# A fused top-32 attention and gated feed-forward on one core: where the weights are split

## The chip, the cores and the metric

The kernel runs on one core of one Trainium2 chip. The metric is the device time of one execution in microseconds. The core's engines run side by side, each through its own instruction queue in order: TensorE (PE in the profile; PEld is its weight load), VectorE (DVE), ScalarE (ACT), GpSimd (POOL) and SyncE (SP), which here only issues DMAs. An engine that has to wait for another one holds up everything behind it in its queue.

## The reference

For 8 batches, 8 heads, 576 positions and head size 64, the attention keeps the 32 largest scores of each row, takes the softmax over them and multiplies by the values. The result, as 4608 rows of 512, goes through a gated feed-forward part of width 1536.

```python
scores = scale * np.matmul(q, k.transpose(0, 1, 3, 2))
kth = np.partition(scores, -top_k, axis=-1)[..., -top_k:-top_k + 1]
attn = softmax over the scores >= kth          # written out in the reference
x = (attn @ v) as [4608, 512]
gate = 1.0 / (1.0 + np.exp(-(x @ w_gate)))
out = (gate * (x @ w_val)) @ w_out
```

All inputs are float32 or wider; the weights arrive with eight bytes per element, as two 32-bit words.

## The kernel before

**Steps.** The attention runs as 160 steps. A step is one tile of up to 128 query rows for one pair of heads (batch `b`, tile `i`, pair `p`). In batch 0 the tiles are grouped (0, 1), (2, 3), (4): eight steps for the first 256 rows, eight for the next 256, four for the last 64. Step numbers `n` below count from 0. Names in the order carry batch, tile and pair: `e_0_2_0` is batch 0, tile 2, pair 0, step n = 8; `e_0_3_0` is n = 9.

In a step, TensorE makes the scores (`pss`), ScalarE writes them to `s` (L259, L281), VectorE takes the largest eight of each segment (`cand`, L340), narrows them (L344, L346), ScalarE and GpSimd build `under` and `u` (L353, L359), VectorE finds the 32nd largest (`kths`, L367) and masks the exponentials (`e`, L294). TensorE transposes `e` (`pt`), ScalarE writes that to `et` (L384, L392, L401), TensorE multiplies with the values (`po`).

**Iterations.** In iteration n of `run`, PE's code has the scores of step n + 2, the transposes of step n - 2 and the value product of step n - 3; `choose(n)` is the VectorE part of step n. PE's instructions stay in the order in which they are written. For the other engines a scheduler sets the order.

**Feed-forward.** The rows are cut in units, the first three of 256 rows, the others of 384. A unit goes through 18 weight tiles in the list `order` (0, 1, 2, 3, 4, 12, 13, 5, ...): gates (`pz`, L455 to L457) and output products (`po2`, L479 to L481). `more(goal)` runs the unit's matmuls until a number of rows is done. `PACE` and `BEHIND` give that number as a function of the attention's rows: nothing before 256 rows; 24 rows of feed-forward at 256 rows of attention, 272 at 512, 512 at 768, 768 at 1184.

**Splitting.** A weight tile has two halves. `split_front` loads the raw words (`wraw`, L149), and makes from the top and the low word a first part and a fraction: ScalarE L156, L161, L165; VectorE L157 to L159; GpSimd L163 twice. `split_back` lets TensorE form the rest (`wrest`, L172 to L174) in the PSUM pool that the gates use too; ScalarE writes it (L176) and stores the half in DRAM (L177). Later units load the stored tiles. Unit 0 uses the first ten weights of `order` from DRAM (`w_first`) and the last eight straight from the split (`wsplit`).

The first ten weights, 20 halves, are split two halves to an iteration in n = 0 to 9 (`fronts`, L629 to L634 and L673 to L684). From n = 10 on `first_weights` and `next_front` (L187 to L203) split the other 16 halves, every third tick at most (L664 to L668).

Of the kernel before, what the change touches and what calls it, by code (L numbers as in the profile page):

```python
# [10 lines left out]
F32 = mybir.dt.float32  # L11
I32 = mybir.dt.int32
U32 = mybir.dt.uint32
F32R = mybir.dt.float32r
BF16 = mybir.dt.bfloat16
FP8 = mybir.dt.float8e4
AF = mybir.ActivationFunctionType
ALU = mybir.AluOpType
# [11 lines left out]
def tile_topk_attention_then_gated_ffn(  # L30
# [8 lines left out]
    nc = tc.nc  # L39
    P = 128  # L40
    B, H, _, S = k.shape
    D = P // 2
    HALF = S // 2
    NP = H // 2
# [3 lines left out]
    FG = NE = NP  # L48
# [13 lines left out]
    EARLY = 2 * P  # L62
# [14 lines left out]
    PACE = [(EARLY, 24), (2 * EARLY, EARLY + 16), (3 * EARLY, 2 * EARLY), (3 * EARLY + BEHIND, 3 * EARLY)]  # L77

    LOADED = 10
# [46 lines left out]
    for name, bufs in (("w", 3), ("f2", 3), ("f4", NE + 1), ("fg", FG + 2)):  # L126
        pools[name] = ctx.enter_context(tc.tile_pool(name=name, bufs=bufs))
# [10 lines left out]
    pre_pools = {n: pre.enter_context(tc.tile_pool(name=n, bufs=bufs)) for n, bufs in (("signs", 1), ("raw", 3), ("parts", 2))}  # L138
    plus, minus = [pre_pools["signs"].tile([P, P], F32R, tag=t, name=t) for t in ("plus", "minus")]
    nc.scalar.activation(plus, ident, AF.Copy, scale=2.0**-52)  # L140
    nc.scalar.activation(minus, ident, AF.Copy, scale=-1.0)

    def split_front(idx, i):

        if i == 0:
            splits[idx] = pools["w"].tile([P, 2, 2, NP, P], F32R, tag="w", name=f"wsplit_{idx}")
        raw = pre_pools["raw"].tile([P, NP * P, 2], U32, tag="raw", name=f"wraw_{idx}_{i}")
        half = slice(i * NP * P, (i + 1) * NP * P)
        nc.sync.dma_start(raw.rearrange("p n t -> p (n t)"), w[idx][:, half].bitcast(U32))  # L149
        low, top = raw[:, :, 0], raw[:, :, 1]  # L150
        pair = splits[idx][:, i].rearrange("p a c n -> p a (c n)")
        lead = pre_pools["parts"].tile([P, NP * P], F32, tag="lead", name=f"wt_lead_{idx}_{i}")
        frac = pair[:, 1]
        lead_u = lead.bitcast(U32)
        with first_scores(idx == i == 0):
            nc.scalar.activation(lead, top.bitcast(F32), AF.Copy, scale=2.0**-112)  # L156
        nc.vector.tensor_scalar(lead_u, lead_u, 3, None, op0=ALU.logical_shift_left)  # L157
        nc.vector.scalar_tensor_tensor(top, top, 0x80000000, lead_u, op0=ALU.bitwise_and, op1=ALU.bitwise_or)
        nc.vector.tensor_scalar(lead_u, top, 0xFF800000, None, op0=ALU.bitwise_and)  # L159
        with first_scores(idx == i == 0):  # L160
            nc.scalar.activation(frac, low, AF.Copy)  # L161
        for c in (slice(0, 2 * P), slice(2 * P, 4 * P)):
            nc.gpsimd.tensor_tensor(frac[:, c], frac[:, c].bitcast(F32), lead[:, c], op=ALU.mult)  # L163
        bits = top.bitcast(F32)
        nc.scalar.activation(pair[:, 0], bits, AF.Copy)  # L165
        waiting.append((idx, i, pair, bits, ticks[0]))
# [354 lines left out]
    def run(general):  # L521
# [109 lines left out]
        for n in range(len(steps) + 3):  # L631
# [3 lines left out]
            if not general and n == LOADED:  # L635
                first_weights(0)
# [19 lines left out]
            else:  # L656
# [26 lines left out]
                if splitting:  # L683
                    split_back()  # L684
# [77 lines left out]
```

## Time and profile before

| | us |
|---|---|
| median of 3 runs | 1614.03 |
| lowest and highest | 1612.47, 1614.16 |
| the profiled execution | 1610.78 |
| its span | 1608.9 |
| PE busy in the span | 1533.2 (95%) |
| DVE, ACT, POOL busy | 1290.7, 1168.9, 1128.9 |

The span runs from the first instruction to the last. Idle time of PE counts only if PE sets the end in that stretch, so the profile is read by stretches: the opening up to the first gate matmul (0 to 141 us), the rest of batch 0 (to 281 us), a stretch after it (to 455 us), and the long remainder.

### The profile page before, as it was taken

To read this page: it belongs to the slowest core of one execution; us is meant where nothing else is said; L and a number is where in the kernel's file an instruction comes from. 1 tells how busy PE (TensorE), PEld (TensorE's weight loads), DVE (VectorE), ACT (ScalarE), POOL (GpSimd) and SP (SyncE) were. 2 spreads that over 40 slices of the span, in tenths; PEclk is the share of its full clock that TensorE was granted. 3 is DMA by queue.
4 is the path that set the end of the run, shared out by engine and by line. 5 is a ranking of instruction groups with operands and counts; after the bars stand their busy time and mean duration, and the time that the engine had idled before them with its cause. 6 is when DMAs were issued, how large, how long until landed. Compare 5 with 4: busy or idle time off the path is not lost.

```text
span 1608.9 us, 36757 instructions
## 1 busy us (share of the span) xinstructions
PE 1533.2 (95%) x11810; PEld 1428.9 (89%) x11810; DVE 1290.7 (80%) x5940; ACT 1168.9 (73%) x2567; POOL 1128.9 (70%) x1747
## 2 busy tenths in 40 slices
PE   5778998989999999999999999999999999999998
PEld 2346877989999999999999999999999999999998
DVE  7997776799999878799989878799989788899101
ACT  6876787778877777877777777877767777777321
POOL 4765796688886885787776885787776886675322
PEclk9888999999999999999999999999999999999999
DMA  8667587776665665565655665565555665555575
GB/s 250 206 198 272 204 286 280 264 250 226 230 212 201 211 238 198 192 225 200 212 207 180 226 229 195 209 225 204 192 200 204 220 217 180 194 195 182 175 278 191
DMA packets 92459, 348.18 MB, mean 216 GB/s; under 512 B 10336, under 2 KB 37472, under 8 KB 63328
## 3 DMA queue, kind: packets, MB, share of 16 engines
q1 hardware_dynamic: 87072, 326.87, 59.0%
q10 hardware_dynamic: 5184, 18.88, 3.0%
q8 instruction: 95, 1.56, 0.4%
q14 instruction: 108, 0.88, 0.2%
HBM read 317.39 MB, written 28.31 MB: 215 GB/s over the span
## 4 chain that ended last, share of the span: by engine, by line
PE 74%; DVE 12%; ACT 4%; POOL 3%; issue 2%; DMA 1%; POOLq 0%; DVEq 0%; ACTq 0%; SPq 0%
PE pz L455 11%; PE pz L457 11%; PE pz L456 11%; PE pss L273 8%; PE po L414 8%; PE pt L378 6%; PE po L479 6%; PE po L481 5%; PE po L480 5%; DVE cand L340 3%; DVE e L294 3%; DVE kths L367 2%; POOL u L359 1%; DVE cand L346 1%; ACT under L353 1%
## 5 line engine op out<-in xcount | busy, mean ns | idle before, releaser
L359 POOL TENSOR_TENSOR u<-s,under 128x288 f32<-128x288 f32 x576 | 421.9, 756 | 94.0 <-ACT under L353 89.8
L455 PE MATMUL pz<-xh,w 128*128 128x384 f32 (+1 forms) x1152 | 405.8, 352 | 1.7 <-ACT xh L421 1.7
L340 DVE MAX8 cand<-s 128x8 f32<-128x72 f32 x2304 | 347.5, 217 | 67.8 <-ACT s L281 56.1
L456 PE MATMUL pz<-xl,w 128*128 128x384 f32 (+1 forms) x1152 | 377.0, 327 | 3.0 <-POOL xl L422 3.0
L457 PE MATMUL pz<-xh,w 128*128 128x384 f32 (+1 forms) x1152 | 377.9, 328 | 0.0
L294 DVE SCALAR_TENSOR_TENSOR e<-s,kths,e 128x576 f32<-128x576 f32 x288 | 285.3, 994 | 29.4 <-ACT e L289 28.9
L353 ACT ACTIVATE under<-s,leads 128x576 fp8e4<-128x576 f32 x288 | 222.4, 773 | 102.7 <-DVE leads L344 94.2
L367 DVE MAX8 kths<-u 128x8 f32<-128x584 f32 x288 | 219.1, 761 | 65.9 <-POOL u L360 63.3
L289 ACT ACTIVATE e<-s,st 128x576 f32<-128x576 f32 x288 | 210.4, 771 | 35.8 <-PE pt L378 21.0
L455 PEld LDWEIGHTS pz<-xh,w 128*128 128x128 f32 x1152 | 217.6, 189 | 6.1 <-issue 2.6
L456 PEld LDWEIGHTS pz<-xl,w 128*128 128x128 f32 x1152 | 218.3, 189 | 3.4 <-POOL xl L422 3.4
L467 POOL TENSOR_TENSOR gl<-gf,gh 128x384 fp32r<-128x384 f32 (+1 forms) x156 | 155.1, 995 | 91.4 <-ACT gh L466 88.1
L457 PEld LDWEIGHTS pz<-xh,w 128*128 128x128 f32 x1152 | 217.1, 188 | 0.0
L384 ACT ACTIVATE et<-pt 128x384 f32<-128x384 f32 (+1 forms) x384 | 196.9, 523 | 19.5 <-PE pt L378 13.7
L479 PE MATMUL po<-gh,w 128*128 128x384 f32 (+1 forms) x576 | 203.2, 353 | 0.1
L378 PE MATMUL pt<-ident,e 128*128 128x128 f32 x1152 | 191.5, 276 | 7.3 <-ACT et L384 7.0
L480 PE MATMUL po<-gl,w 128*128 128x384 f32 (+1 forms) x576 | 188.3, 327 | 2.6 <-POOL gl L467 2.6
L481 PE MATMUL po<-gh,w 128*128 128x384 f32 (+1 forms) x576 | 188.5, 327 | 0.0
L414 PEld LDWEIGHTS po<-et,v 128*64 128x64 f32 x1600 | 163.8, 139 | 17.0 <-issue 12.7
L414 PE MATMUL po<-et,v 128*64 128x128 f32 (+1 forms) x1600 | 177.1, 268 | 0.0
L415 PE MATMUL po<-et,v 128*64 128x128 f32 (+1 forms) x1600 | 177.1, 268 | 0.0
L281 ACT ACTIVATE s<-pss 128x576 f32<-128x576 f32 x256 | 165.1, 645 | 8.6 <-PE pss L273 8.3
(110 smaller groups left out, 3457.1 us busy)
## 6 DMA issues: line engine op xcount, KB each, us to landing
w<-ws SPq DMA_DIRECT2D x216, 1024.0 KB, 4.9
v<-in_v_dram SPq DMA_DIRECT2D x68, 320.0 KB, 3.6
wraw<-in_w_dram SPq DMA_DIRECT2D x36, 512.0 KB, 4.4
ws<-wsplit ACTq DMA_DIRECT2D x36, 512.0 KB, 4.4
qraw<-in_q_dram SPq DMA_DIRECT2D x140, 128.0 KB, 3.4
kraw<-in_k_dram SPq DMA_DIRECT2D x56, 288.0 KB, 3.7
w_first<-ws SPq DMA_DIRECT2D x10, 1024.0 KB, 4.9
out_dram<-acc SPq DMA_DIRECT2D x40, 192.0 KB, 4.0
```

The lines of the kernel that those rows point to most:

```text
L294: nc.vector.scalar_tensor_tensor(e[:, j], s[:, j], kth[j], e[:, j], op0=ALU.is_ge, op1=ALU.mult, accum_out=st[:, 4 + j : 5 + j])
L340: nc.vector.max(cand[:, j, 8 * g : 8 * g + 8], s[:, j, g * SEG : (g + 1) * SEG])
L359: nc.gpsimd.tensor_tensor(u[:, j, c], s[:, j, c], under[:, j, c], op=ALU.mult)
L367: nc.vector.max(kths[:, at[j] : at[j] + 8], u[:, j])
L378: nc.tensor.transpose(pt[:, c], ef[:, k0 : k0 + P], ident)
L414: nc.tensor.matmul(po[D:, c], vt[:, 5 + a], et[:, 4 + a, :n], start=a == 0, stop=a == 4)
L455: nc.tensor.matmul(ps[:, R], wt[:, u, 0, d], xh[:, R], start=d == 0, stop=False)
L456: nc.tensor.matmul(ps[:, R], wt[:, u, 0, d], xl[:, R], start=False, stop=False)
L457: nc.tensor.matmul(ps[:, R], wt[:, u, 1, d], xh[:, R], start=False, stop=d == NP - 1)
L479: nc.tensor.matmul(ps[:, R], wts[e // 2][:, e % 2, 0, f], gh[:, R], start=f == 0, stop=False)
L480: nc.tensor.matmul(ps[:, R], wts[e // 2][:, e % 2, 0, f], gl[:, R], start=False, stop=False)
L481: nc.tensor.matmul(ps[:, R], wts[e // 2][:, e % 2, 1, f], gh[:, R], start=False, stop=f == FG - 1)
```

## The change

Ten halves, not 20, are split in the iterations n = 0 to 9, one in each; the other 26 are split while unit 0 runs. Up to three halves may be between front and back. The raw load of a half is issued with the front of the half ahead of it. The first part goes to its own tile `wbits` and no longer back into `wraw`; VectorE's third operation reads the upper 16 bits of it at a stride of two and writes a 16-bit `wpower`, which GpSimd multiplies with. The feed-forward pace becomes 16 rows at 256, 232 at 512, 480 at 768, 768 at 1184. The pools change: `parts` 2 to 3 buffers, `power` 1 new, `fg` 6 to 5. `after` has its lines 11 further down: L168, L173, L176 and L187 there are L156, L161, L165 and L176 here.

```diff
-    PACE = [(EARLY, 24), (2 * EARLY, EARLY + 16), (3 * EARLY, 2 * EARLY), (3 * EARLY + BEHIND, 3 * EARLY)]
-    LOADED = 10
+    PACE = [(EARLY, 16), (2 * EARLY, EARLY - 24), (3 * EARLY, 2 * EARLY - 32), (3 * EARLY + BEHIND, 3 * EARLY)]
+    LOADED = 5
-    for name, bufs in (("w", 3), ("f2", 3), ("f4", NE + 1), ("fg", FG + 2)):
+    for name, bufs in (("w", 3), ("f2", 3), ("f4", NE + 1), ("fg", FG + 1)):
...
-        raw = pre_pools["raw"].tile([P, NP * P, 2], U32, tag="raw", name=f"wraw_{idx}_{i}")
-        half = slice(i * NP * P, (i + 1) * NP * P)
-        nc.sync.dma_start(raw.rearrange("p n t -> p (n t)"), w[idx][:, half].bitcast(U32))
+        at = halves_of_weights.index((idx, i))
+        for ahead in halves_of_weights[at : at + 2]:
+            if ahead not in raws:
+                load_raw(*ahead)
...
-        nc.vector.scalar_tensor_tensor(top, top, 0x80000000, lead_u, op0=ALU.bitwise_and, op1=ALU.bitwise_or)
-        nc.vector.tensor_scalar(lead_u, top, 0xFF800000, None, op0=ALU.bitwise_and)
+        nc.vector.scalar_tensor_tensor(word, top, 0x80000000, word, op0=ALU.bitwise_and, op1=ALU.bitwise_or)
+        nc.vector.tensor_scalar(power.bitcast(U16), heads, 0xFF80, None, op0=ALU.bitwise_and)
...
-            nc.gpsimd.tensor_tensor(frac[:, c], frac[:, c].bitcast(F32), lead[:, c], op=ALU.mult)
+            nc.gpsimd.tensor_tensor(frac[:, c], frac[:, c].bitcast(F32), power[:, c], op=ALU.mult)
...
-            if not general and n == LOADED:
+            if not general and n == NP * len(groups[0][1]) + 2:
...
-                        if due and ticks[0] % 3 == 0:
+                        if due and len(waiting) < 3:
                             next_front()
...
-                    if t == 2 and splitting:
-                        if len(waiting) > splitting:
-                            split_back()
-                        if splitting:
-                            split_front(*fronts.pop(0))
+                    if t == 2 and splitting and len(waiting) > 1:
+                        split_back()
...
-                if splitting:
-                    split_back()
```

ScalarE's queue at the very start, in the order before. `s` is the scores of the first two steps, `wraw_1_0` the raw words of the third half; what an instruction waits for stands in brackets:

```order
L259 ACTIVATE s_0_1_0_186<-pss_0_1_0_0_187 128x2x288 [waits PE_49]
L156 ACTIVATE wt_lead_0_0_198<-wraw_0_0_196 128x512 [waits DMAHW5_49]
L161 ACTIVATE wsplit_0_195<-wraw_0_0_196 128x512
L259 ACTIVATE s_0_1_0_186<-pss_0_1_0_1_191 128x2x288 [waits PE_49]
L353 ACTIVATE under_0_0_0_231,sums_0_0_0_228<-s_0_0_0_177,leads_122 128x576 [waits DVE_49,Activation_49]
L165 ACTIVATE wsplit_0_195<-wraw_0_0_196 128x512 [waits DVE_49]
L353 ACTIVATE under_0_0_0_231,sums_0_0_0_228<-s_0_0_0_177,leads_122 128x576
L289 ACTIVATE e_0_0_0_229<-s_0_0_0_177,st_0_0_0_227 128x576 [waits Pool_49]
L289 ACTIVATE e_0_0_0_229<-s_0_0_0_177,st_0_0_0_227 128x576
L156 ACTIVATE wt_lead_0_1_275<-wraw_0_1_273 128x512 [waits DMAHW6_49]
L161 ACTIVATE wsplit_0_195<-wraw_0_1_273 128x512
L161 ACTIVATE wsplit_1_294<-wraw_1_0_295 128x512 [waits DMAHW7_49]
```

The same place of ScalarE's queue in the changed kernel:

```order
L270 ACTIVATE s_0_1_0_189<-pss_0_1_0_0_190 128x2x288 [waits PE_49]
L168 ACTIVATE wbits_0_0_203<-wraw_0_0_199 128x512 [waits DMAHW5_49]
L173 ACTIVATE wsplit_0_198<-wraw_0_0_199 128x512
L173 ACTIVATE wsplit_1_363<-wraw_1_0_283 128x512 [waits DMAHW7_49]
L270 ACTIVATE s_0_1_0_189<-pss_0_1_0_1_194 128x2x288 [waits PE_49]
L364 ACTIVATE under_0_0_0_237,sums_0_0_0_234<-s_0_0_0_180,leads_122 128x576 [waits DVE_49,Activation_49]
```

The instruction that needs the third half's raw words stood eight places behind the second eviction of `s_0_1_0`; now it stands right ahead of it.

TensorE's queue in unit 0, at the gates of weight 4, the fifth of `order`, before:

```order
L455 MATMUL pz_0_1_0_0_1803<-xh_0_0_730,w_first_4_1647 128x256
L456 MATMUL pz_0_1_0_0_1803<-xl_0_0_731,w_first_4_1647 128x256
L457 MATMUL pz_0_1_0_0_1803<-xh_0_0_730,w_first_4_1647 128x256
L455 MATMUL pz_0_1_0_0_1803<-xh_0_1_988,w_first_4_1647 128x256
L456 MATMUL pz_0_1_0_0_1803<-xl_0_1_989,w_first_4_1647 128x256
L457 MATMUL pz_0_1_0_0_1803<-xh_0_1_988,w_first_4_1647 128x256
L378 MATMUL pt_0_2_1_0_1811<-ident_105,e_0_2_1_1414 128x128 x3
```

And in the changed kernel, where weight 12, the sixth, is being split there:

```order
L466 MATMUL pz_0_1_0_0_1688<-xh_0_0_659,w_first_4_1498 128x256
L467 MATMUL pz_0_1_0_0_1688<-xl_0_0_660,w_first_4_1498 128x256
L468 MATMUL pz_0_1_0_0_1688<-xh_0_0_659,w_first_4_1498 128x256
L183 MATMUL wrest_12_0_1692<-wbits_12_0_1546,ident_105 128x512
L184 MATMUL wrest_12_0_1692<-wsplit_12_1543,minus_166 128x512
L185 MATMUL wrest_12_0_1692<-wsplit_12_1543,plus_165 128x512
L266 MATMUL pss_0_2_3_1_1710<-k_0_3_6_378,q_0_2_3_1248 128x288 x2
L466 MATMUL pz_0_1_0_0_1688<-xh_0_1_884,w_first_4_1498 128x256
```

Weight 12, the sixth of `order`, is now the first that is split in use; before it was weight 8, the eleventh. Counted over the whole order, PE's rows up to the first gate matmul are the same but for 30 `wrest` matmuls fewer (30 instead of 60). From there to the last transposes of batch 0 (step n = 19) there are 30 more (78 instead of 48) and 66 gate matmuls fewer (309 instead of 375).

## Rows read from the trace of the kernel before

**Rows 1.** The page: busy time of each engine (share of the span) xinstructions.

```profile
PE 1533.2 (95%) x11810; PEld 1428.9 (89%) x11810; DVE 1290.7 (80%) x5940; ACT 1168.9 (73%) x2567; POOL 1128.9 (70%) x1747
```

**Rows 2.** Windows: stretch and length, busy time by engine, granted clock, DMA share, GB/s.

```profile
0.00:20.00 20.00, 6.65 (x20) 2.54 (x20) 10.40 (x65) 11.77 (x22) 5.99 (x23) 1.00 0.88 251
20.00:141.00 121.00, 86.50 (x411) 46.83 (x412) 111.94 (x464) 96.03 (x189) 82.02 (x119) 0.82 0.67 226
141.00:281.00 140.00, 130.58 (x986) 109.39 (x987) 104.81 (x391) 105.05 (x229) 100.68 (x145) 1.00 0.73 255
281.00:341.00 60.00, 60.00 (x597) 58.94 (x596) 49.90 (x254) 48.19 (x119) 43.17 (x77) 1.00 0.73 260
341.00:455.00 114.00, 104.47 (x974) 100.04 (x973) 107.36 (x551) 93.51 (x214) 96.87 (x154) 0.99 0.67 233
455.00:1590.00 1135.00, 1131.90 (x8756) 1098.42 (x8755) 902.99 (x4215) 812.82 (x1795) 798.14 (x1231) 1.00 0.60 208
```

**Rows 3.** By line: duration ns min/median/max, first and last start, forms.

```profile
L157 DVE TENSOR_SCALAR wt_lead<-wt_lead x36: 401/454/920, 13.3 to 244.9; 128x512 uint32<-128x512 uint32 x36
L158 DVE SCALAR_TENSOR_TENSOR wraw<-wraw,wt_lead x36: 667/738/1228, 13.8 to 245.4; 128x512 uint32<-128x512 uint32 x36
L159 DVE TENSOR_SCALAR wt_lead<-wraw x36: 401/437/922, 14.5 to 246.1; 128x512 uint32<-128x512 uint32 x36
...
L163 POOL TENSOR_TENSOR wsplit<-wsplit,wt_lead x72: 720/736/1295, 15.1 to 251.0; 128x256 fp32r<-128x256 f32 x72
```

**Rows 4.** The page's groups: GpSimd with a one-byte second operand: busy, mean ns.

```profile
L359 POOL TENSOR_TENSOR u<-s,under 128x288 f32<-128x288 f32 x576 | 421.9, 756 | 94.0 <-ACT under L353 89.8
```

**Rows 5.** Timeline of PE around the first gate matmul: start, length, instruction, idle before.

```profile
129.25 2.08 PE L172 MATMUL wrest<-wraw,ident 128*128 128x512 f32 x2 [6.06 <-DVE wraw L158]
...
139.40 0.87 PE L378 MATMUL pt<-ident,e 128*128 128x128 f32 x6
140.20 0.76 PE L255 MATMUL pss<-k,q 64*128 64x288 f32 x4
140.89 0.55 PE L378 MATMUL pt<-ident,e 128*128 128x128 f32 x3
141.27 0.27 PE L381 MATMUL pt<-ident,inv 128*128 128x128 f32 x1
141.30 0.36 PE L455 MATMUL pz<-xh,w_first 128*128 128x256 f32 x1
```

**Rows 6.** Timeline of DVE: the second mask of step n = 8 (`e_0_2_0`).

```profile
108.31 0.81 DVE L294 SCALAR_TENSOR_TENSOR e<-s,kths,e 128x576 f32<-128x576 f32 x1
```

**Rows 7.** Timeline of ACT at the start.

```profile
11.95 0.65 ACT L161 ACTIVATE wsplit<-wraw 128x512 fp32r<-128x512 uint32 x1
12.93 0.65 ACT L259 ACTIVATE s<-pss 128x576 f32<-128x576 f32 x1 [0.32 <-PE pss L255]
```

**Rows 8.** The raw loads issued in the first 20 us: third issue, then landing times.

```profile
L149 SPq DMA_DIRECT2D wraw<-in_w_dram x3: 430/432/583, 3.7 to 9.5; - x3
...
DMA to landing us min/median/max: 4.5/6.3/7.4
```

**Rows 9.** Timeline of PE at 190 us: one half's rest between gate matmuls.

```profile
189.84 0.28 PE L456 MATMUL pz<-xl,w_first 128*128 128x256 f32 x1
189.96 0.28 PE L457 MATMUL pz<-xh,w_first 128*128 128x256 f32 x1
190.08 1.06 PE L172 MATMUL wrest<-wraw,ident 128*128 128x512 f32 x2
190.55 0.82 PE L173 MATMUL wrest<-wsplit,minus 128*128 128x512 f32 x1
191.21 0.40 PE L174 MATMUL wrest<-wsplit,plus 128*128 128x512 f32 x1
191.44 0.28 PE L455 MATMUL pz<-xh,wsplit 128*128 128x256 f32 x1
```

**Rows 10.** Timeline of ACT: transposes of steps n = 9 and n = 19 written out.

```profile
156.61 0.57 ACT L384 ACTIVATE et<-pt 128x512 f32<-128x512 f32 x1
...
281.08 0.56 ACT L401 ACTIVATE et<-pt 64x128 f32<-64x128 f32 x2
```

**Rows 11.** The longest of PE's waits from 141 to 281 us: total, times, longest.

```profile
PE wrest L174 <- POOL wsplit L163: 3.2, 3, 2.0
PE po L480 <- POOL gl L467: 1.5, 1, 1.5
```

**Rows 12.** ACT's operations of a half, 20 to 141 us: xcount, busy us, mean ns, idle before.

```profile
L165 ACT ACTIVATE wsplit<-wraw 128x512 fp32r<-128x512 f32 x19 | 12.9, 679 | 8.2 <-DVE wraw L158 8.2
L156 ACT ACTIVATE wt_lead<-wraw 128x512 f32<-128x512 f32 x19 | 12.8, 674 | 6.0 <-POOL wsplit L163 5.6 <-DMA wraw<-in_w_dram 0.4
L176 ACT ACTIVATE wsplit<-wrest 128x512 fp32r<-128x512 f32 x20 | 11.9, 593 | 0.2 <-PE wrest L174 0.2
L161 ACT ACTIVATE wsplit<-wraw 128x512 fp32r<-128x512 uint32 x17 | 11.5, 679 | 2.3 <-DMA wraw<-in_w_dram 2.0 <-issue 0.2
```

More of the change, by code (lines that the diff above doesn't have):

```diff
@@ L13 @@
 U32 = mybir.dt.uint32
+U16 = mybir.dt.uint16
 F32R = mybir.dt.float32r
@@ L137, in tile_topk_attention_then_gated_ffn @@
     pre = ExitStack()
-    pre_pools = {n: pre.enter_context(tc.tile_pool(name=n, bufs=bufs)) for n, bufs in (("signs", 1), ("raw", 3), ("parts", 2))}
+    pre_pools = {n: pre.enter_context(tc.tile_pool(name=n, bufs=bufs)) for n, bufs in (("signs", 1), ("raw", 3), ("parts", 3), ("power", 1))}
     plus, minus = [pre_pools["signs"].tile([P, P], F32R, tag=t, name=t) for t in ("plus", "minus")]
@@ L141, in tile_topk_attention_then_gated_ffn, with load_raw @@
     nc.scalar.activation(minus, ident, AF.Copy, scale=-1.0)
+    halves_of_weights = [(t, i) for t in order for i in range(2)]
+    raws = {}
+    def load_raw(idx, i):
+        raws[idx, i] = raw = pre_pools["raw"].tile([P, NP * P, 2], U32, tag="raw", name=f"wraw_{idx}_{i}")
+        nc.sync.dma_start(raw.rearrange("p n t -> p (n t)"), w[idx][:, i * NP * P : (i + 1) * NP * P].bitcast(U32))
     def split_front(idx, i):
@@ L146, in split_front @@
             splits[idx] = pools["w"].tile([P, 2, 2, NP, P], F32R, tag="w", name=f"wsplit_{idx}")
-        raw = pre_pools["raw"].tile([P, NP * P, 2], U32, tag="raw", name=f"wraw_{idx}_{i}")
-        half = slice(i * NP * P, (i + 1) * NP * P)
-        nc.sync.dma_start(raw.rearrange("p n t -> p (n t)"), w[idx][:, half].bitcast(U32))
+        at = halves_of_weights.index((idx, i))
+        for ahead in halves_of_weights[at : at + 2]:
+            if ahead not in raws:
+                load_raw(*ahead)
+        raw = raws[idx, i]
         low, top = raw[:, :, 0], raw[:, :, 1]
         pair = splits[idx][:, i].rearrange("p a c n -> p a (c n)")
-        lead = pre_pools["parts"].tile([P, NP * P], F32, tag="lead", name=f"wt_lead_{idx}_{i}")
+        bits = pre_pools["parts"].tile([P, NP * P], F32, tag="bits", name=f"wbits_{idx}_{i}")
         frac = pair[:, 1]
-        lead_u = lead.bitcast(U32)
+        word = bits.bitcast(U32)
+        power = pre_pools["power"].tile([P, NP * P], BF16, tag="power", name=f"wpower_{idx}_{i}")
+        heads = bits.bitcast(U16).rearrange("p (n t) -> p n t", t=2)[:, :, 1]
         with first_scores(idx == i == 0):
-            nc.scalar.activation(lead, top.bitcast(F32), AF.Copy, scale=2.0**-112)
-        nc.vector.tensor_scalar(lead_u, lead_u, 3, None, op0=ALU.logical_shift_left)
-        nc.vector.scalar_tensor_tensor(top, top, 0x80000000, lead_u, op0=ALU.bitwise_and, op1=ALU.bitwise_or)
-        nc.vector.tensor_scalar(lead_u, top, 0xFF800000, None, op0=ALU.bitwise_and)
+            nc.scalar.activation(bits, top.bitcast(F32), AF.Copy, scale=2.0**-112)
+        nc.vector.tensor_scalar(word, word, 3, None, op0=ALU.logical_shift_left)
+        nc.vector.scalar_tensor_tensor(word, top, 0x80000000, word, op0=ALU.bitwise_and, op1=ALU.bitwise_or)
+        nc.vector.tensor_scalar(power.bitcast(U16), heads, 0xFF80, None, op0=ALU.bitwise_and)
         with first_scores(idx == i == 0):
@@ L162, in split_front @@
         for c in (slice(0, 2 * P), slice(2 * P, 4 * P)):
-            nc.gpsimd.tensor_tensor(frac[:, c], frac[:, c].bitcast(F32), lead[:, c], op=ALU.mult)
-        bits = top.bitcast(F32)
+            nc.gpsimd.tensor_tensor(frac[:, c], frac[:, c].bitcast(F32), power[:, c], op=ALU.mult)
         nc.scalar.activation(pair[:, 0], bits, AF.Copy)
```

## The prediction

> **What bounds the kernel now.** I read the engines' shares first, then the busy time by stretches, then the timelines at the stretches' borders and PE's waits. PE is busy for 95% of the span [rows 1], but that is an average. By stretches [rows 2]: from 455 to 1590 us PE is busy for 1131.9 of 1135 us, and nothing there can be won. All else lies ahead of it. From 0 to 141 us PE is busy for 6.7 + 86.5 us and idle for 48; VectorE, at 111.9 of the 121 us after the first 20, is the bound. From 141 to 281 us PE is busy for 130.6 of 140 and sets the pace, with 9.4 us of waits. From 281 to 341 us it is never idle. From 341 to 455 us PE (104.5 of 114) and VectorE (107.4) share the bound, and PE is idle for 9.5 us. At the border, PE waits 6.06 us for VectorE's part of a late half, and the first gate matmul starts at 141.30 [rows 5], although the mask of step n = 8, the last attention result that stands ahead of it in PE's order, was done at 109.1 [rows 6]. So the splits, not the attention, opened the feed-forward part.
>
> The sums are made against the profiled execution, 1610.78 us, which lies 3.25 under the median of the runs, 1614.03. Its span is 1608.9; the 1.9 around it is left as it is.
>
> **The opening.** A half costs VectorE 0.45 + 0.74 + 0.44 = 1.63 us [rows 3]. In the new order 11 halves instead of 16 stand ahead of the second mask of n = 8: 5 x 1.63 = 8.2 us less. Some VectorE work of the following step is drawn ahead of it, though; over all rows up to that mask, by kind and duration, I count 4 us less.
>
> Against it stands the start. In ScalarE's queue the instruction that needs the third raw load has moved ahead of the second eviction of step 1. The load is issued at 9.5 us in a full DMA queue (share 0.88) and lands up to 7.4 us later, near 16.9 [rows 2, 8]. As many loads are ahead of it as before. ScalarE was free for that eviction at 12.6 and ran it at 12.93 [rows 7]; it would now run at about 17. Behind the waiting instruction are that eviction, `under` and the first exponentials; VectorE waits for the eviction and GpSimd for `under`. Cost 4 us, bounds 0 (should the load land early) and 5.
>
> So the mask of n = 8 stays at about 109.1. From there PE has the transposes, a score block and the last weight's rest that stands ahead anyway: 1.9 us at full clock [rows 5], 4 at half. I add 2 for ScalarE's further waits for raw loads, which the scheduler moved early as well. First gate matmul at 115: **26 us earlier than 141.3**.
>
> **What is not done yet by then.** PE's rows up to that point differ by 30 `wrest` matmuls, ten halves. At full clock a half takes 191.44 - 190.08 = 1.36 us of PE [rows 9]: 13.6 us that now lie in a stretch where PE is the bound. In exchange the slower pace leaves out 66 gate matmuls up to the end of batch 0. They start 0.12 us apart (189.84, 189.96) [rows 9]: 7.9 us less.
>
> **New waits.** VectorE's rows from the mask of n = 8 to that of n = 9 come to 10.7 us, so that one is done near 121 to 123. PE has 16 rows of feed-forward until then, 16 x 432 / 256 = 27 matmuls or 3.2 us. It waits 5 us (0 to 8). In the rest of batch 0 PE's 9.4 us of waits belong to 16 halves in use; the longest is for GpSimd's product of a half [rows 11]. With 26 halves, in proportion, 5.9 us more. But half of the weights had their second half's rest directly ahead of their first use, and now at least 2.4 us of other PE work stands between. I take 3 (bounds -3 and 9).
>
> **The sum up to the end of batch 0.** The transposes of n = 19 were out at 281.6 [rows 10]. Now 281.6 - 26.2 + 13.6 - 7.9 + 5 + 3 = 269.1: **12.5 us earlier**.
>
> **What is owed.** The 7.9 us of gates are made up until 1184 rows. Seven rows, 1.4 us, fall to 281 to 341 us, where PE has no idle time: paid in full. The other 6.5 us fall where PE is idle for 9.5 us but VectorE is 94% busy [rows 2]; I let half be hidden, 3.2 (bounds 0 and 6.5). Owed: 4.6.
>
> Net -12.5 + 4.6 = -7.9 us: 1602.9 in the profiled execution's terms, **1606** as a median.
>
> **Edits taken at nothing.** VectorE's third operation, 512 two-byte words read at a stride of two, is not in the trace. Its nearest rows are the one-input operations at 0.40 to 0.45 us and the two-input one at 0.74 [rows 3]; I take 0.44, since it too has one tensor input. At 0.74 it costs 0.3 x 36 = 11 us of VectorE, of which 4 lie in the opening on the path; the rest has VectorE's idle 35 us of the 140 as cover. At 0.40 it gains 0.5 there. GpSimd's product with a two-byte operand: 736 ns for 256 columns with four-byte operands [rows 3], 756 for 288 with a one-byte one [rows 4], so 0.67 to 0.74; no change, covered by GpSimd's 39 us of idle time in 141 to 281. `wbits` apart from `wraw` changes no length and frees the raw buffer earlier; if the raw tile were late still, it is ScalarE's wait counted above. One `fg` buffer less: a buffer comes back five gate tiles later, when PE has at least one tile (24 matmuls, 2.9 us) behind its last reader; without that cover up to 3 us for each of the early reuses. On SP the second raw load now stands ahead of the next pair's keys and queries; they come later by at most the spread of the landings, 2.9 us [rows 8], and PE then waits for ScalarE in any case.
>
> **The clock.** From 20 to 141 us the granted clock is 0.82, from 141 on 1.00: both levels, 1.2 and 2.4 GHz, occur in the opening [rows 2]. With ten rests fewer, at some 2 us each there, PE would be busy for 66 of 95 us, 70%, against 71% now: I expect the same mixture. The Trainium skill ("TensorE: Matmul & The Clock Gate", Part 1, on the clock gate) says that the throttled level is the default and activity releases it. By that, fewer matmuls between gaps speak against the change; by the trace so far only the share of busy time can be compared.
>
> **Rivals.**
> - *ScalarE's queue sets the rest of batch 0 (slower).* A half costs it 0.68 + 0.67 + 0.59 + 0.68 = 2.6 us [rows 12]. It was busy for 105 of the 140 us; ten halves more make 131, in the 154 us from 115 to 269: 85%. Nowhere in rows 2 does it pass 82%. Were 80% its limit, the end of batch 0 is at 115 + 164 = 279, only 2.6 us earlier, and with all 7.9 us owed paid the kernel is 5 us slower: 1619. It decides once ScalarE's work passes about 80% of that stretch. Against it: its idle time there is mostly waiting for others, and it never was the bound.
> - *The opening keeps its length.* ScalarE meets each early raw load before the attention's evictions, as at the start, two or three more times at up to 3 us. The feed-forward opens near 122 and the net is about -1: 1613.
> - *The opening falls to 1.2 GHz throughout (slower).* 66 us of PE at 0.82 become 108, 13 more than the 95 there are: net +5, 1619. For it: less work for each step; against it: the unchanged busy share.
> - *The waits do not come.* No wait for the mask, none added in use, the debt hidden: -7.9 - 8 - 3.2 = -19, 1595.
>
> **How the numbers follow.** What cannot be told from no change is 0.2%, 3.2 us; the three runs span 1.7. Forecast 0.42 (0.37 faster, 0.04 same, 0.01 slower); no waits 0.12, all faster; opening unchanged 0.18 (0.03, 0.12, 0.03); ScalarE 0.20 (0, 0.03, 0.17); clock 0.08 (0, 0.01, 0.07). Together faster 0.52, same 0.20, slower 0.28. The forecast's own range, from the bounds of the waits, the debt and VectorE's third operation, is 1597 to 1614. To leave out no more than 2 in 10 it reaches to the slower rivals: 1597 to 1620.
>
> **What would show it.** The eviction at 12.93 is late by 4 us and waits for a raw load. The first gate matmul starts near 115, with 30 `wrest` matmuls ahead of it. The last transposes of batch 0 are out near 269. PE's idle time between the first gate matmul and there is some 17 us, for masks and halves. From 341 to 455 us its idle time is halved. From 500 us on both traces run alike, shifted. It is wrong if the first gate matmul comes after 125, if ScalarE or GpSimd is the name on most of PE's new waits for over 15 us, or if the end of batch 0 is not earlier than 281.

## The result and the profile after

The changed kernel takes **1595.92 us** (median of 4 runs, 1595.09 to 1597.74), the kernel before 1613.53 beside it: a ratio of 0.9893, 95% interval 0.9876 to 0.9910, or 17.6 us less. A second set of runs gave 0.9901 (0.9887 to 0.9915). The forecast was 1606, with a range from 1597 to 1620: the direction was right, the size was not.

The profiled execution has a span of 1595.9 us. The page's first row answers to [rows 1]: TensorE has the same 11810 instructions and is busy 10.6 us less.

```profile
PE 1522.6 (95%) x11810; PEld 1427.3 (89%) x11810; DVE 1285.6 (81%) x5940; ACT 1165.3 (73%) x2567; POOL 1124.2 (70%) x1747
```

The windows, cut at the first gate matmul, the end of batch 0 and steps n = 27 and n = 40, with the columns of [rows 2] (length, busy time of PE, PEld, DVE, ACT, POOL, granted clock, DMA share, GB/s):

```profile
0.00:20.00 20.00, 5.73 (x18) 2.46 (x20) 6.96 (x45) 6.51 (x11) 2.51 (x18) 1.00 0.89 234
20.00:111.80 91.80, 62.61 (x378) 36.25 (x377) 89.83 (x429) 75.95 (x153) 58.15 (x91) 0.89 0.52 180
111.80:265.90 154.10, 140.53 (x993) 113.10 (x992) 127.97 (x460) 127.86 (x274) 124.33 (x179) 0.98 0.73 253
265.90:324.60 58.70, 58.70 (x574) 57.76 (x573) 47.83 (x253) 47.79 (x120) 40.25 (x72) 1.00 0.74 265
324.60:439.70 115.10, 109.50 (x1029) 106.38 (x1028) 108.31 (x552) 92.18 (x214) 98.78 (x156) 0.99 0.73 253
439.70:1577.00 1137.30, 1132.53 (x8756) 1098.66 (x8756) 901.34 (x4201) 813.50 (x1797) 798.10 (x1233) 1.00 0.59 207
```

In the second row VectorE is idle for 2.0 us of 91.8; before, it was idle for 9.1 of 121 [rows 2]. In the third, TensorE is idle for 13.6 us. A profiled execution of the second set (changed_again) has the same points at 111.8, 264.7 and 438.3 us, so 1 to 2 us between two kernels at such a point say nothing. The next rows are TensorE's around the first gate matmul, which came at 141.30 before [rows 5], and VectorE's second mask of n = 8, which began at 108.31 [rows 6]:

```profile
111.79 0.27 PE L392 MATMUL pt<-ident,inv 128*128 128x128 f32 x1
111.82 0.36 PE L466 MATMUL pz<-xh,w_first 128*128 128x256 f32 x1
...
102.30 1.25 DVE L305 SCALAR_TENSOR_TENSOR e<-s,kths,e 128x576 f32<-128x576 f32 x1
```

This mask is done at 103.55, where it was done at 109.12. From 20 us to there, before and then after:

```profile
20.00:109.12 89.12, 65.21 (x278) 33.93 (x278) 86.09 (x348) 73.74 (x145) 63.02 (x90) 0.83 0.62 207
```

```profile
20.00:103.55 83.55, 54.57 (x315) 30.81 (x313) 81.58 (x385) 71.25 (x144) 55.57 (x85) 0.90 0.54 187
```

ScalarE's start answers to [rows 7]. The copy that needs the third raw load waits 5.64 us, and the eviction behind it starts at 18.90 instead of 12.93:

```profile
12.03 0.66 ACT L173 ACTIVATE wsplit<-wraw 128x512 fp32r<-128x512 uint32 x1
18.34 0.66 ACT L173 ACTIVATE wsplit<-wraw 128x512 fp32r<-128x512 uint32 x1 [5.64 <-DMA wraw<-in_w_dram]
18.90 0.64 ACT L270 ACTIVATE s<-pss 128x576 f32<-128x576 f32 x1
```

VectorE's third operation, on two-byte words at a stride, takes 426 ns in the median; 0.44 was taken, from [rows 3]:

```profile
L171 DVE TENSOR_SCALAR wpower<-wbits x36: 398/426/946, 14.6 to 241.9; 128x512 uint16<-128x512 uint16 x36
```

And the last transposes of batch 0, at 281.08 before [rows 10], are written out at

```profile
265.37 0.55 ACT L412 ACTIVATE et<-pt 64x128 f32<-64x128 f32 x2
```

So the profiled execution gains 15.7 us up to the end of batch 0, keeps 15.4 of it at n = 40 (439.7 against 455.1), and loses 2.4 in the rest of the span.

### The profile page after: what moved, and what is told of

It reads as the page before. It is cut to its first block, busy times and chain, and to the rows that moved or that the text cites. A ratio compares the mean times of both kernels' runs of the same rounds, so it can differ in the third digit from the quotient of the medians.

```text
span 1595.9 us, 36725 instructions
## 1 busy us (share of the span) xinstructions
PE 1522.6 (95%) x11810; PEld 1427.3 (89%) x11810; DVE 1285.6 (81%) x5940; ACT 1165.3 (73%) x2567; POOL 1124.2 (70%) x1747
## 4 chain that ended last, share of the span: by engine, by line
PE 69%; DVE 10%; ACT 3%; POOL 2%; issue 2%; DMA 1%; SPq 0%; ACTq 0%; POOLq 0%; DVEq 0%
PE pz L466 10%; PE pz L468 10%; PE pz L467 10%; PE pss L284 8%; PE po L425 7%; PE pt L389 6%; PE po L490 5%; PE po L492 5%; PE po L491 5%; DVE cand L351 3%; DVE e L305 2%; DVE kths L378 2%; DVE cand L357 1%; PE pt L400 1%; ACT under L364 1%
## 5 line engine op out<-in xcount | busy, mean ns | idle before, releaser
L300 ACT ACTIVATE e<-s,st 128x576 f32<-128x576 f32 x288 | 210.5, 771 | 34.3 <-PE pt L389 18.8
L425 PEld LDWEIGHTS po<-et,v 128*64 128x64 f32 x1600 | 160.4, 137 | 16.5 <-issue 11.6
L425 PE MATMUL po<-et,v 128*64 128x128 f32 (+1 forms) x1600 | 173.5, 265 | 0.0
L426 PE MATMUL po<-et,v 128*64 128x128 f32 (+1 forms) x1600 | 173.5, 265 | 0.0
L389 PEld LDWEIGHTS pt<-ident,e 128*128 128x128 f32 x1152 | 146.0, 141 | 30.4 <-ACT et L395 12.7
```

The lines of the kernel that those rows point to most:

```text
L389: nc.tensor.transpose(pt[:, c], ef[:, k0 : k0 + P], ident)
L425: nc.tensor.matmul(po[D:, c], vt[:, 5 + a], et[:, 4 + a, :n], start=a == 0, stop=a == 4)
```

## The experiments

Four parts were taken apart: the **placement** (five weights, one half per step), the **split** (words and power in tiles of their own, load ahead, one gate buffer less), the **pace** table, and the **rule in use** (fewer than three in flight). All ratios are to the kernel before on the same chip; the medians come from several chips, on which the kernel before had 1611.7 to 1613.5. "Gate" is the first gate matmul, "batch 0" the last transposes of batch 0 (n = 19), both as points of time, and "28-39" the time between the last transposes of n = 27 and of n = 40. All three are from the run's profiled execution.

| kernel | gate | batch 0 | 28-39 | median us | ratio (95%) |
|---|---|---|---|---|---|
| before | 141.3 | 281.6 | 114.1 | 1613.5 | 1 |
| changed | 111.8 | 265.9 | 115.1 | 1595.9 | 0.9893 (0.9876-0.9910) |
| changed_again | 111.8 | 264.7 | 114.9 | 1596.2 | 0.9901 (0.9887-0.9915) |
| place_alone | 111.0 | 283.4 | 113.5 | 1611.5 | 0.9996 (0.9987-1.0005) |
| pace_alone | 140.0 | 280.9 | 115.0 | 1609.2 | 0.9980 (0.9969-0.9992) |
| split_alone | 129.4 | 275.1 | 115.8 | 1603.1 | 0.9943 (0.9926-0.9959) |
| place_pace | 111.7 | 278.6 | 119.7 | 1606.6 | 0.9968 (0.9956-0.9980) |
| old_place | 128.6 | 264.1 | 119.9 | 1597.4 | 0.9910 (0.9896-0.9923) |
| old_place_14 | 128.6 | 262.3 | 115.1 | 1592.5 | 0.9874 (0.9857-0.9890) |
| old_pace | 111.9 | 274.4 | 113.2 | 1602.3 | 0.9940 (0.9924-0.9957) |
| old_ticks | 112.0 | 266.0 | 115.0 | 1596.4 | 0.9899 (0.9883-0.9916) |
| no_ahead | 111.3 | 263.8 | 116.9 | 1595.7 | 0.9896 (0.9880-0.9911) |
| in_place | 113.2 | 269.4 | 120.8 | 1604.7 | 0.9940 (0.9925-0.9955) |
| bits_two | 114.1 | 269.8 | 115.7 | 1599.1 | 0.9917 (0.9904-0.9930) |
| raw_four | 138.6 | 281.1 | 113.1 | 1608.3 | 0.9972 (0.9962-0.9982) |
| no_stall | 106.6 | 260.0 | 118.8 | 1593.6 | 0.9889 (0.9874-0.9904) |
| no_stall_all | 107.6 | 261.7 | 115.6 | 1592.7 | 0.9878 (0.9864-0.9893) |
| no_stall_no_ahead | 104.8 | 258.3 | 120.1 | 1594.2 | 0.9887 (0.9873-0.9901) |
| no_stall_slower | 107.5 | 263.5 | 120.0 | 1598.3 | 0.9916 (0.9903-0.9929) |
| best_14 | 107.3 | 259.9 | 115.0 | 1591.2 | 0.9870 (0.9854-0.9887) |

**The placement, undone and alone.** old_place puts `LOADED = 10`, the second `split_front` of a step and the old `split_back` calls back into the changed kernel; place_alone takes the same lines of the changed kernel into the one before.

> The changed kernel with only the placement undone: ten weights, two halves in each of the first ten steps, the gates called at step 10, as before; the new form of the split, the raw load one half ahead, three in flight and the slower pace stay. Theory A (how many halves stand ahead of the gates decides, all else is small): the first gate matmul is back near 140 us and the time near that of the kernel before, 1610 to 1616, with the slower pace perhaps 2 above it. Rival B (the new form of the split and the raw loads ahead make the opening short): first gate matmul before 125 us, time 1596 to 1602.

> The kernel before with only the placement changed: five weights, one half per step, the gates called at step 10; old form of the split, no raw load ahead, old pace, old rule in use. Theory A: first gate matmul at 110 to 118 us and the time within 4 us of the changed kernel, 1594 to 1601. Rival B: first gate matmul after 125 us, because raw loads and the split's operations come late, and 1606 to 1614. A third reading (placement opens early, but halves in use at the old rule are late) would show the first gate matmul before 118 us, more than 20 us of waits of TensorE for rests from there to the last transposes of batch 0, and 1600 to 1606.

Theory A, which was the prediction's, fell on both. In old_place theory B has the time (1597.4) but not the opening, which comes at 128.6 and not before 125. place_alone opens the gates at 111.0, as A said, and is not faster: from there to the end of batch 0 it needs 172.4 us. Its windows, and TensorE's two longest waits in the second one (total, times, longest):

```profile
20.00:111.00 91.00, 63.38 (x377) 37.46 (x375) 89.12 (x419) 76.27 (x151) 58.84 (x91) 0.89 0.53 181
111.00:283.40 172.40, 153.65 (x1028) 122.89 (x1029) 130.67 (x459) 130.29 (x278) 125.06 (x179) 0.94 0.71 241
...
PE po L479 <- ACT acc L488: 5.9, 1, 5.9
PE wrest L174 <- POOL wsplit L163: 3.7, 3, 2.4
```

Against the 140.3 us before, that is 32 us more: 13.6 for the ten halves [rows 9], 9.4 of further idle time (18.8 against 9.4) and the rest, 9, at the granted clock of 0.94, since it was 1.00 in that stretch before [rows 2]. All that the early gate won (30.3) goes there. The third reading, late halves, missed as well: TensorE's waits ahead of rests come to 5.9 us there, not to over 20, and the time is 1611.5.

**The split and the pace, alone.** split_alone takes the new `split_front`, its pools and `fg` into the kernel before, pace_alone only the line `PACE`.

> The kernel before with only the new split: word and power in tiles of their own, three of them, so that a raw buffer is free after VectorE's second operation and not after TensorE's rest; the raw load one half ahead; one gate buffer less. Ten weights, two halves per step, the old pace and the old rule in use stay. Theory S (raw buffers that waited for TensorE are what made the opening long before: the load of raw words waited 28.8 us for TensorE's rests there): first gate matmul near 128.6, as in the run with only the placement undone, so 12 us before 141.3; the end of batch 0 is 270 to 274 and the time 1601 to 1606. Rival T (an earlier opening is given back in full to waits and to a lower clock, as with the placement alone): end of batch 0 within 3 us of 281.6, time 1609 to 1614.

> The kernel before with only the pace table changed. Theory E: nothing changes up to 141 us; 66 gate matmuls fewer bring the end of batch 0 from 281.6 to 272 to 275, and the time to 1603 to 1606, since the gates left out are done where TensorE is idle. Rival U (owed gates are paid in full after batch 0): end of batch 0 near 274 but step n = 40 within 2 us of 455.1, time 1610 to 1614.

Theory S held, with the end of batch 0 1.1 us beyond its bounds: the split alone wins 0.57%, 9.2 us. What it frees stands in SyncE's queue, where L149 is the load of raw words. From 20 to 141 us, before and then with the new split at the old placement (old_place), as waiting engine, line, releaser: us in total, times, longest:

```profile
SPq L149 <- PE wrest L172: 28.8, 17, 5.9
SPq L149 <- DVE wt_lead L159: 24.3, 6, 7.6
```

```profile
SPq L149 <- DVE wbits L170: 52.3, 16, 5.9
```

Before, TensorE's rest was the last reader of a raw buffer, so the next load, and with it VectorE, stood behind TensorE's order; now VectorE's own second operation gives the buffer back. These waits are as long in all (53.1 and 52.3 us), but for another engine. With that, the ten weights are through and the gates open at 128.6 instead of 141.3:

```profile
20.00:128.60 108.60, 81.30 (x415) 44.07 (x415) 106.10 (x444) 92.86 (x186) 76.43 (x108) 0.87 0.73 241
```

VectorE is idle for 2.5 us in this window, 9.1 before. That is half of the 12.7 us; the other half is VectorE work that no longer stands ahead of the gates (106.1 us against 111.9), a change of order that these runs do not tell apart from the buffers.

pace_alone is 0.2% faster, too little for theory E and, by 0.8 us, too much for rival U, for which batch 0 also ends too late. There are 66 gate matmuls fewer, yet TensorE is busy almost as long as before (129.7 us against 130.6 [rows 2]), at a lower clock:

```profile
140.00:280.90 140.90, 129.69 (x953) 107.87 (x952) 100.07 (x403) 107.09 (x227) 96.25 (x149) 0.95 0.69 236
```

**The pace and the rule, undone.** One line each: `PACE` as before; `if due and ticks[0] % 3 == 0`.

> The changed kernel with only the pace table undone (24, 272, 512 for the due rows of the first three units instead of 16, 232, 480). The four runs so far let theory A fall: the placement alone opens the gates at 111 us and wins nothing, since from there to the last transposes of batch 0 TensorE needs 172.4 us instead of 140.3. Theory E (the slower pace takes 66 gate matmuls, 7.9 us, out of the stretch where TensorE is the bound and they cost nothing later, where TensorE is idle anyway): the end of batch 0 is 8 us or more later than 265.9, 274 to 280, step n = 40 some 6 to 10 us later than 439.7, and the time 1602 to 1606. Rival F (the gates only fill waits): end of batch 0 within 3 us of 265.9, time 1595 to 1599.

> The changed kernel with only the rule in use undone: a new half is begun every third tick instead of whenever fewer than three are in flight. Theory G (three in flight is what spares TensorE the waits for halves in use): TensorE's idle time from the first gate matmul to the last transposes of batch 0 rises from 13.6 us to 18 or more, the end of batch 0 is 5 us or more later, and the time 1600 to 1606. Rival H (the rule hardly matters, since a half needs more than three ticks anyway): the same stretch within 3 us of 154.1, time 1595 to 1599.

Beside the new split the pace is worth 8.5 us at the end of batch 0 and 6 to 8 in all: E held here, as it did not alone. With the old split it brings the end of batch 0 forward by 4.8 us at the new placement (place_alone 283.4, place_pace 278.6) and by 0.7 at the old one. The rule in use does nothing (rival H).

**The load ahead** (`halves_of_weights[at : at + 1]`):

> The changed kernel with the raw words loaded in the step that splits them, not one half ahead. The third raw load still has 15 transfers ahead of it, so the stall at the start stays. Theory A: the splits of the opening stand behind a step of VectorE work and the loads are hidden anyway: first gate matmul within 2 us of 111.8; in use a load that takes 4.5 to 7.4 us comes late for some halves, 1 to 4 us more of waits by TensorE up to the end of batch 0; time 1596 to 1600. Rival D (the load ahead is what keeps VectorE busy): VectorE idle for over 8 us between 36 and 113 us, first gate matmul after 118, time 1603 or more.

It does nothing either: the gates open where A said, and the 1 to 4 us of further waits that A expected do not come (1595.7).

**Both pieces of the prediction together, without the split**: place_pace, the kernel before with the new placement and pace.

> The kernel before with the new placement and the new pace table, but the old split and the old rule in use. Theory S (the new split is needed where halves are split in use, too; the old one makes them late and TensorE's clock drop): first gate matmul at 111, the end of batch 0 not before 274, time 1604 to 1609. Rival V (placement and pace are enough together, as the prediction had it): end of batch 0 at 266 to 270, time 1596 to 1600.

Theory S held, V fell: 0.32% faster of the 1.07%. Its profiled execution took 1612.9 us, 6.3 more than the median of its seven runs (1604.3 to 1612.9). The opening and the rest of batch 0 in it:

```profile
20.00:111.70 91.70, 60.83 (x376) 34.61 (x375) 89.83 (x420) 76.27 (x151) 58.92 (x91) 0.96 0.53 180
111.70:278.60 166.90, 150.05 (x991) 119.06 (x992) 127.58 (x466) 130.03 (x274) 125.54 (x179) 0.92 0.69 232
```

In the second window TensorE's waits ahead of a half's rest come to 14.5 us; they are 9.6 in the changed kernel and 13.7 in in_place, below. Twice such a wait and a fall of the clock come one behind the other. Two windows, the rows that start the falls, and between them a third wait:

```profile
170.00:180.00 10.00, 8.71 (x58) 6.43 (x58) 7.01 (x12) 5.02 (x12) 9.43 (x14) 0.66 0.78 294
220.00:230.00 10.00, 10.00 (x33) 7.85 (x32) 6.49 (x22) 6.02 (x12) 8.41 (x12) 0.54 0.35 118
...
170.87 1.88 PE L172 MATMUL wrest<-wraw,ident 128*128 128x512 f32 x2 [1.83 <-DVE gf L465]
206.96 1.17 PE L172 MATMUL wrest<-wraw,ident 128*128 128x512 f32 x2 [2.34 <-ACT wsplit L176]
218.22 1.49 PE L172 MATMUL wrest<-wraw,ident 128*128 128x512 f32 x2 [2.45 <-ACT wsplit L176]
220.50 1.81 PE L273 MATMUL pss<-k,q 64*128 64x288 f32 x3
```

After waits of 1.83 and 2.45 us the granted clock is 0.66 and 0.54 over ten us, the latter close to the lower of its two levels, 1.2 GHz. TensorE is then busy, but for less work. Not every such wait does it: behind the one of 2.34 us the first two matmuls of the rest take 1.17 us, near the 1.06 of [rows 9], and the clock of 200 to 210 us is 1.00.

**Which part of the split.** raw_four gives the kernel before a fourth raw buffer (`("raw", 4)`, `fg` and `bqr` one less); bits_two the changed kernel two word tiles (`("parts", 2)`); in_place holds the raw buffer again:

```
-        nc.vector.scalar_tensor_tensor(word, top, 0x80000000, word, ...)
+        nc.vector.scalar_tensor_tensor(top, top, 0x80000000, word, ...)
...
-        heads = bits.bitcast(U16).rearrange("p (n t) -> p n t", t=2)[:, :, 1]
+        heads = raw.bitcast(U16)[:, :, 3]
...
+        bits = top.bitcast(F32)
```

> The kernel before with four raw buffers instead of three; one gate buffer and one query buffer of the odd batches less make room. The split, the placement, the pace and the rule in use are those of before. Theory S1 (the new split wins by giving raw buffers back early; its other parts win nothing): a fourth buffer does part of the same, loads of raw words wait for TensorE's rests for less than 15 us instead of 28.8 up to 141 us, VectorE's idle time from 20 us to the first gate matmul falls from 9 us to 5 or less, the first gate matmul comes at 128 to 136, and the time is 4 to 9 us lower, 1603 to 1608. Rival S2 (it is the order of VectorE's instructions, or the two-byte operation, that wins): first gate matmul within 3 us of 141.3 and 1610 to 1614.

> The changed kernel with two tiles for the words of a half instead of three. They are free only after TensorE's rest. Theory S1: VectorE (through ScalarE's first copy of a half) waits for TensorE's rests again; first gate matmul 2 to 8 us later than 111.8, TensorE's idle time from there to the end of batch 0 over 16 us, time 1599 to 1606. Rival W (two are enough, since a half needs under two steps from its first copy to its rest): first gate matmul within 1 us, time 1594 to 1598.

> The changed kernel with VectorE's second operation writing the words back over the raw ones, as before, so that a raw buffer is free only after TensorE's rest has read it; the two-byte third operation and its two-byte product, the placement, the pace, the rule in use and the load ahead stay. Theory S1 (giving the raw buffer back early is the part of the new split that counts): loads of raw words wait for TensorE again, for over 30 us in 20 to 111 us; the stretch from the first gate matmul to the end of batch 0 is 160 us or more instead of 154.1, by more waits and a lower granted clock; time 1602 to 1608, near the placement and the pace with the old split, 1606.6. Rival Y (the two-byte operations or the order that comes with them win): time 1594 to 1598.

raw_four is half a hit for S1: VectorE's idle time falls to 4.3 us and the kernel gains 0.28%, but the loads still wait 31.4 us for TensorE and the gate moves by only 2.7 us, which is within rival S2's bounds. bits_two is as S1 said at the gate (2.3 us later) and at its lower end in time; TensorE's idle time did not rise. in_place has S1's time, 8.5 us over the changed kernel, and its waits, but not its reason: the stretch behind the gates takes 156.2 us, not 160, at a clock of 0.99:

```profile
SPq L149 <- PE wrest L184: 48.6, 10, 8.8
...
113.20:269.40 156.20, 140.81 (x988) 110.54 (x987) 125.21 (x450) 127.50 (x270) 120.61 (x176) 0.99 0.72 249
328.70:449.50 120.80, 112.45 (x1027) 108.58 (x1025) 109.77 (x545) 94.42 (x219) 99.25 (x157) 0.96 0.70 242
```

The gates open only 1.4 us later, though the loads wait 48.6 us for TensorE, and only 3.5 to 4.7 us of the 8.5 are there at the end of batch 0. The rest comes from 329 to 450 us, where no weight is split: 120.8 us instead of 115.1.

**An order far behind the change.** That stretch takes 115 to 117 us in some kernels with the new pace and 118.8 to 120.8 in the others. Between the first masks of `e_1_1_0` and `e_2_0_0`, VectorE's order is one and the same, 399 rows, in changed, old_ticks, no_ahead, bits_two, pace_alone and no_stall_all; in old_place, place_pace, in_place, no_stall and no_stall_no_ahead it is another, 410 rows, the same in these five but for a few rows in its first half. no_stall_slower (120.0), with a pace table of its own, has a third. In old_place_14 and best_14 the first number of `PACE` is 14 instead of 16, which gives the first order; best_14 is otherwise no_stall_no_ahead, below.

> The run with only the placement undone (ten weights, two halves per step), and the first number of its pace table 14 instead of 16. That number changes no work, but with it the scheduler's order of VectorE and ScalarE in the second half of batch 1 (steps 28 to 39, where no weight is split) is row for row the changed kernel's. With 16 it was the other one, and that stretch took 119.9 us instead of 115.1. Theory O (that order alone makes 4 to 5 us, and the placement is worth nothing): the stretch takes 115 to 116 us, the end of batch 0 stays near 264, time 1592 to 1595, not above the changed kernel's. Rival (the stretch is long for what was left undone before it, not for its order): the stretch 119 us or more, 1596 to 1599.

> The changed kernel without the stall at the start, with the raw words loaded in the step that splits them, and 14 for 16 as in the run beside it, which gives the changed kernel's order in steps 28 to 39. Theory O: end of batch 0 near 258 as without the 14, steps 28 to 39 in 115 to 116 us instead of 120.1, time 1588 to 1591, the fastest of all. Rival: 1592 to 1595, as without it.

Theory O held in the stretch (115.1 and 115.0 us) and in old_place_14's time; best_14's time, 1591.2, lies just above its bounds. old_place, then old_place_14, each from the gate to the end of batch 0 and in steps 28 to 39:

```profile
128.60:264.10 135.50, 128.42 (x952) 108.33 (x951) 106.81 (x425) 105.99 (x231) 102.35 (x157) 0.95 0.74 254
322.80:442.70 119.90, 111.28 (x1027) 107.42 (x1026) 109.61 (x545) 94.24 (x219) 99.31 (x157) 0.97 0.70 243
```

```profile
128.60:262.30 133.70, 125.84 (x954) 105.01 (x953) 108.18 (x426) 105.65 (x232) 103.40 (x157) 0.99 0.73 258
321.00:436.10 115.10, 109.54 (x1029) 106.39 (x1028) 108.33 (x552) 92.31 (x214) 98.77 (x156) 0.99 0.72 253
```

With the same order behind it, the old placement is not slower than the new one: 1592.5 us, ratio 0.9874. The new placement opens 16.8 us earlier and needs 20.4 more from there (154.1 against 133.7: 14.7 more of busy TensorE and 5.7 of idle). Whether it costs something in the end, the intervals leave open.

**The stall at the start.** no_stall orders one copy behind the eviction; no_stall_all does it for all halves of the opening (`evicted[2 * at - 1]`); no_stall_no_ahead adds to no_stall that a load is not ahead; no_stall_slower adds a slower pace.

```
-        with first_scores(idx == i == 0):
+        with tc.issue_after(evicted[3].ins) if at == 2 else first_scores(idx == i == 0):
             nc.scalar.activation(frac, low, AF.Copy)
```

> The changed kernel with one order added: the ScalarE copy that needs the third raw load is issued only after the second eviction of step 1 has been placed. Theory A (VectorE bounds the whole opening, so what it loses at the start is lost at the gates): the eviction is back at 12.9 us, VectorE's idle 4.58 us ahead of 19.57 is gone, the first gate matmul comes 4 to 5 us earlier, near 107, and the time is 4 to 5 us lower, 1591 to 1592. Rival C (the early step is made up later, because VectorE or GpSimd waits for loads in the next steps): first gate matmul within 1 us of 111.8, time 1595 to 1597.

> The changed kernel in which each ScalarE copy that needs a raw load in the opening is issued behind the second eviction of the step two ahead. Theory A2 (every wait of ScalarE for a raw load there moves the gates): both waits are gone, the 5.64 us at 18.34 and the 1.99 us at 32.62, the first gate matmul comes at 105 to 107, the end of batch 0 near 260 and the time is 1 to 3 us under the changed kernel's, 1592 to 1595. Rival Z (the copies are now late for GpSimd's product, and TensorE waits for it): first gate matmul after 108, time 1595 to 1599.

> The changed kernel without the stall at the start and with the raw words loaded in the step that splits them. The load ahead made no difference by itself (1595.7 without it). If that holds without the stall as well: first gate matmul at 106 to 108, time 1592 to 1595. If the stall had hidden the late loads: first gate matmul after 109, time 1595 to 1599.

> The changed kernel without the stall at the start and with a pace slower still: 8, 192 and 432 due rows for the first three units instead of 16, 232 and 480, so some 70 gate matmuls fewer up to the end of batch 0. Theory E2 (what is put off still finds idle time of TensorE from 319 to 437 us, 8.2 us there): end of batch 0 at 250 to 254 instead of 260.0, step n = 40 at 431 to 436, time 1587 to 1591. Rival X (that idle time is VectorE's to give and is used up): end of batch 0 near 252, step n = 40 within 2 us of 437.5 and time 1592 to 1596.

Without the stall the gate comes 5.2 us earlier and the end of batch 0 5.9. no_stall then gives 3.7 back by the other order (118.8), and its time misses theory A's by 1.6 us; no_stall_all, whose gate at 107.6 is 0.6 later than its theory had it, keeps the first order and wins 3.4 us over changed_again on the same chip. no_stall_no_ahead opens the gates at 104.8, earlier than expected, has the other order as well (120.1) and its time as expected. no_stall_slower misses both its theories and loses 4 to 5 us on no_stall: with fewer gates to do, batch 0 ends 3.5 us later, and TensorE is idle for 17.6 us from the gates to there (14.1 in no_stall). So the loss is there before anything that was put off is done; its cause was not traced. best_14 is the fastest, 1591.2 us, and beats the kernel before by 1.3%; its interval overlaps one of the changed kernel's two and touches the other, so the 4 to 5 us between the medians are likely, not shown; old_place_14 is no different from it.

## Why the prediction was wrong

- **The step that failed** is "Edits taken at nothing": `wbits` apart from `wraw` "changes no length and frees the raw buffer earlier", and stood in the sum with nothing. The split that it belongs to is the largest single gain: 9.2 us alone. Beside the placement and the pace it takes the ratio from 0.9968 (place_pace) to 0.9893 and 0.9901, which is 11 to 12 us; in the profiled executions 4.6 of them are the order in steps 28 to 39 (119.7 against 115.1). I costed the lengths of operations, not whose order a buffer waited for. How much of it is the buffer is shown in part: in_place undoes that alone, and batch 0 ends 3.5 to 4.7 us later.
- *Where it counts*: at the old placement ahead of the gates, at the new one behind them. With the old split they open at 111.0 (place_alone) and 111.7 (place_pace), with VectorE idle for 1.9 us in both. From there on the forecast had a full clock and 17.4 us of idle time. With the old split these came to 18.8 and 16.9 us, at clocks of 0.94 and 0.92; with the new one to 13.6 us at 0.98. Which waits the old split costs differs: those ahead of rests are 14.5 us in place_pace and 5.9 in place_alone.
- *VectorE bounds the opening*: right up to the mask of n = 8. Of its 9.1 us of idle time before, 6.0 lie behind that mask, where TensorE waited 6.06 us for a late half [rows 5]. *The stall*: right in its place, 4 us taken, 5.97 measured.
- *First gate matmul at 115*: 111.8. The mask was left at 109.1, with 4 us less work and 4 us of stall. It was done at 103.55: from the start to it VectorE worked 88.5 us instead of 96.5, so 8 us less and not 4, and it was idle for 2.0 us instead of 3.0 from 20 us on. From the mask to the gate it then took 8.3 us, not 5.9.
- *The credit*: "26 us earlier" was laid on the placement. That one gives 30 us at the gate and takes all of it back (place_alone); the end of batch 0 comes no earlier by it at the same split and pace (old_place 264.1, changed 265.9). So the direction was right in part by luck: the split and the pace won, not the placement. place_pace, which leaves the split out, has the forecast's 1606 as its time, but batch 0 ends at 278.6 in it, not at 269.1.
- *From the gate to the end of batch 0*, 154.1 predicted (269.1 less 115) and measured. That is luck, since two errors cancel: waits for mask and halves came to 13.6 us of idle time, not 17.4, and TensorE was busy for 140.5 us, not some 137, most of it by the clock of 0.98. The 9.4 us of waits before, which the prediction gave to the halves, stood ahead of rests for 5.6 us only.
- *What is owed*, 4.6 us: 0.3 from the end of batch 0 to n = 40. The pace is worth its gates beside the new split (8.5 us of batch 0), less with the old one (4.8 and 0.7).
- *The sum*: 3.2 at the gate and 4.3 of the debt make 7.5 us; 2.4 lost behind n = 40 make it 5.1, which is what the profiled execution (1597.7) differs from the 1602.9 forecast. The last 4.6 us of the miss are where the profiled executions lie: 2.75 under the median before, 1.8 above it after. The 2.4 us were not traced to a cause; behind n = 40 the profiled executions of the table need 1152.7 to 1156.2 us.
- *Rivals*: the opening did not keep its length. ScalarE at 83% (127.9 of 154.1) did not set the stretch. In the opening the clock rose. "The waits do not come", 1595, had the time, by a hidden debt as it said, but TensorE's idle time rose by 4.2 us instead of staying, so it had it by luck.

## What to carry to other kernels

Ask for every staging buffer who reads it last: if that is an engine that runs in another order, the next load stands in that order too, and a split whose last read is on another engine was worth 9.2 us here without removing any work. An earlier start is worth nothing where the work that was moved behind it takes as long: 30.3 us were won at the gates by the placement alone, and 32 lost from there on. Before a part of a change is credited, run it alone and run the rest without it; a scheduler can flip an order far behind, so compare stretch by stretch.

## What the runs showed of the hardware

- The granted clock is not read off the busy share. In the opening it rose from 0.82 to 0.89, a mixture of its two levels, 1.2 and 2.4 GHz, while TensorE's busy share fell from 71% to 68%. The same matmuls are busy for longer at a lower clock (the first two of a rest 1.06 us at 190.08 [rows 9], 1.88 at 170.87 in place_pace), and busy time times clock rose from 59% to 61% of the stretch. Kernels with the new placement had from 0.84 (bits_two) to 0.96 (place_pace) there. The Trainium skill ("TensorE: Matmul & The Clock Gate", Part 1, on the clock gate) says that activity releases the throttle. These stretches neither show that nor speak against it.
- Waits of 1.8 and 2.5 us ahead of rests were followed by ten us at 0.66 and 0.54 in place_pace; one of 2.3 us in the same execution was not.
- 14 for 16 due rows, with the same work in all, changed steps 28 to 39 from 119.9 to 115.1 us together with the scheduler's order there. In the 14 profiled executions with one of these two orders, the first goes with 114.9 to 116.9 us and the other with 118.8 to 120.8.
